# dS of two key chunks by one VectorE operation of 1000 columns

## The chip, the cores and the metric

The kernel runs on one core of a Trainium2 chip. The metric is the device time of one execution in microseconds (us), the median of several runs. The core has five engines with a queue each: TensorE (PE, its weight loads PEld), VectorE (DVE), ScalarE (ACT), GpSimd (POOL) and SyncE (SP), which here only issues DMAs. Matmuls write into PSUM, which has banks of 512 float32 columns per partition; DVE and ACT read it from there into SBUF.

## The reference

The program is one branch-former layer with its whole backward pass: attention on one side, a gated local branch with a depthwise convolution on the other, a merge of both, and the gradients of the input and of seven weights. There are 2 batches of 4000 tokens with 144 channels, in bfloat16. Cut to the part that matters here:

```python
B, T, D, K = (2, 4000, 144, 5)
qkv = jnp.einsum('btd,de->bte', _layernorm(x), w_qkv)
q, k, v = (qkv[..., :D].copy(), qkv[..., D:2 * D].copy(), qkv[..., 2 * D:].copy())
scores = jnp.einsum('btd,bsd->bts', q, k) * D ** (-0.5)
p = _softmax(scores, axis=-1)
attn = jnp.einsum('bts,bsd->btd', p, v)
...
_out, _vjp = jax.vjp(_f, x, w_qkv, w_att_out, w_mlp_in, dw_csgu, w_mlp_out, dw_merge, w_merge)
_grads = _vjp(grad_out)
```

The backward pass of the softmax is dS = P * (dP - delta), where dP is the gradient that arrives at P and delta is one number per query. It is this product that the change touches.

## The kernel before

The kernel handles the batches one after the other. For each there is a preparation (layer norm, transposes), the attention phase, in which forward and backward are fused, and a merge phase. The attention phase takes most of the time. It runs over 32 query tiles of 125 tokens (`PB`); the 4000 keys are 8 chunks of 500 columns (`CH`), handled as 4 pairs of chunks. In one step of the loop over `t` there are 8 slots:

- Slots 0 to 3 make the scores of tile `t` (`S_pair`). Four matmuls of 500 columns (L683, L684) fill a PSUM tile `ps` of two banks. One DVE operation over both banks (L688 for the first pair, L690 for the others) finds a running minimum of the negated scores, and one ACT operation (L691) writes the exponentials into `Pbuf`.
- After slot 3 `rescale` brings the first three pairs of chunks to a common maximum (two DVE operations L700, one of ACT L702), and a DMA transposes P into `PT` (L703). `Y_half` (L711) multiplies PT with the tokens in slots 2 and 3 of the next step.
- Slots 4 to 7 make dS of tile `t - 1` (`dP_pair`). Four matmuls (L733, L734) fill a `ps` tile with dP, and DVE subtracts delta, multiplies with P and writes dS into `Sbuf` (L739). At the end of the step a DMA transposes dS into `ST` (L859), which `Z_half` (L755) reads a step later.
- In most slots one `X_group` runs: matmuls (L794) of dS and P of tiles `t - 2` and `t - 3` into a PSUM tile `X`, and a DVE addition into `acc` (L800). Small pieces of the local branch (`units`) are spread over the slots by count.

The `ps` tiles of `S_pair` and `dP_pair` come from one pool with two buffers of two banks each; `X` and the small pieces share a pool of three buffers. The columns of P and dS lie in blocks of 125 with a stride of 128, so 500 columns are 4 rows of 125, and 1000 are 8. L739 stands in a loop over the two halves of the pair, each of which reads one bank:

```python
for h in range(2):
    c = 2 * c2 + h
    psrc = Pbuf[0:PB, i % NPB, c * 512:(c + 1) * 512]...
    sdst = Sbuf[0:PB, i % NDB, c * 512:(c + 1) * 512]...
    nc.vector.scalar_tensor_tensor(sdst, ps[:, h, 0:CH]..., DL[i][:], psrc, op0=ALU.subtract, op1=ALU.mult)
```

The source gives the order of the work by its slots. The framework in which the kernel is written puts the instructions into the engines' queues and sets the waits, and it may place an instruction ahead of an earlier one that is not ready by its reckoning. In the trace of before the two L739 of a pair follow each other directly in 214 of 256 pairs; in the other 42 another DVE operation stands between them. The tile `ps` is released as a whole.

Of the kernel before, what the change touches and what calls it, by code (L numbers as in the profile page):

```python
# [10 lines left out]
ALU = mybir.AluOpType  # L11
# [5 lines left out]
PB = 125  # L17
CH = 500
# [597 lines left out]
def phase_att(k, W, b, S, A, M):  # L616
    nc, tc = k.nc, k.tc
# [3 lines left out]
    NPB, NDB = 4, 3  # L621
    es_loc, es_sg = ExitStack(), ExitStack()
    with ExitStack() as es:
# [5 lines left out]
        Pbuf = ab.tile([128, NPB, GW], BF, name="Pbuf")  # L629
        Sbuf = ab.tile([128, NDB, GW], BF, name="Sbuf")  # L630
# [14 lines left out]
        QT, QB, RL, DL, YZ, ZN, ZT, NM, DHT = {}, {}, {}, {}, {}, {}, {}, {}, {}  # L645
# [24 lines left out]
        def pchunk(pb, c2):  # L670
            return Pbuf[0:PB, pb, c2 * 1024:(c2 + 1) * 1024]
# [55 lines left out]
        def dP_pair(i, c2):  # L727
            qt = QT[i]
            ps = ps_sg.tile([PB, 2, 512], F32, tag="sg")
            for h in range(2):  # L730
                c = 2 * c2 + h
                cs = slice(c * CH, (c + 1) * CH)
                nc.tensor.matmul(ps[:, h, 0:CH], qt[:, 2, :], xaTm[:, cs], start=True, stop=False)  # L733
                nc.tensor.matmul(ps[:, h, 0:CH], qt[:, 3, :], R[:, cs], start=False, stop=True)  # L734
            for h in range(2):
                c = 2 * c2 + h
                psrc = Pbuf[0:PB, i % NPB, c * 512:(c + 1) * 512].rearrange("p (a b) -> p a b", b=128)[:, :, 0:PB]
                sdst = Sbuf[0:PB, i % NDB, c * 512:(c + 1) * 512].rearrange("p (a b) -> p a b", b=128)[:, :, 0:PB]
                nc.vector.scalar_tensor_tensor(sdst, ps[:, h, 0:CH].rearrange("p (a b) -> p a b", b=PB), DL[i][:], psrc, op0=ALU.subtract, op1=ALU.mult)  # L739

        def last_tr(c2):

# [73 lines left out]
        for t in range(NB + 1):  # L816
# [9 lines left out]
            for s in range(8):  # L826
                if s < 4 and ok(t):
                    S_pair(t, s)
                if s >= 4 and ok(t - 1):
                    dP_pair(t - 1, s - 4)  # L830
# [630 lines left out]
```

## Time and profile before

| what | value |
|---|---|
| median of 3 runs | 1478.05 us (1475.49 to 1479.26) |
| the profiled execution, its own time | 1477.11 us |
| its span, first to last instruction | 1475.3 us |
| mean granted TensorE clock | 0.985 |
| busy: PE, DVE, ACT, POOL | 1377.6, 1217.1, 849.7, 282.0 us |
| attention phases in the span | about 60 to 660 us and 770 to 1373 us |

The profile is of one execution. A group of instructions is named by its line, engine, operation and the tiles that it writes and reads (out<-in), with its shape and count; behind the bar stand its busy time in us, the mean duration of one in ns, and the idle time of its engine just before such instructions, with what ended most of it ("<-PE ps L734" is the matmul of line 734). In a timeline the columns are start, duration, engine, line, operation; "x2" joins two neighbours into one row, and the bracket has the idle time of the engine before it. DVE operations overlap a little: the next one starts before the one before has quite ended, so an operation holds the engine for less than its duration.

### The profile page before, as it was taken

The numbers are of one execution on the slowest core, as the hardware profiler recorded it, in microseconds if no ns is written. First come the engines' busy times: TensorE is split into PE (matmuls) and PEld (weight loads), VectorE is DVE, ScalarE is ACT, GpSimd is POOL, SyncE is SP. The second block draws the span as 40 slices with busy tenths as digits, with TensorE's granted clock in tenths as the row PEclk, the third lists the DMA queues.
The fourth block names the chain that finished last, engine by engine and source line by source line (L and its number), as shares of the span: only waits on it lengthen the run. The fifth ranks groups of instructions, "written<-read, shape, count | busy, mean of one in ns | idle before, by whom it ended". The sixth has DMA issues, their size and how long they took to land. (4 is left out here: it accounts for less than half of the span.)

```text
span 1475.3 us, 39163 instructions
## 1 busy us (share of the span) xinstructions
PE 1377.6 (93%) x16184; PEld 1181.5 (80%) x16184; DVE 1217.1 (82%) x3060; ACT 849.7 (58%) x1538; POOL 282.0 (19%) x494
## 2 busy tenths in 40 slices
PE   2789999999999999997888999999999999999898
PEld 1568888888888888887885888888888888888797
DVE  6699888988898988887638998889898889888754
ACT  1666666666566656632637666666566656555182
POOL 8210111010111110026521112120101010101420
PEclk9899999999999999998999999999999999999999
DMA  3176667666666765578225776677667666677812
GB/s 101 31 144 121 121 121 122 120 122 117 118 115 113 119 118 111 107 138 209 62 56 104 138 122 113 111 121 124 119 123 121 121 121 121 116 117 124 218 35 64
DMA packets 559360, 170.44 MB, mean 116 GB/s; under 512 B 542443, under 2 KB 554093, under 8 KB 559136
## 3 DMA queue, kind: packets, MB, share of 16 engines
q1 hardware_dynamic: 553338, 155.43, 57.1%
q0 software_dynamic: 4768, 12.14, 3.2%
q8 instruction: 126, 2.06, 0.6%
q10 hardware_dynamic: 1076, 0.38, 0.1%
q14 instruction: 52, 0.43, 0.1%
HBM read 21.07 MB, written 14.16 MB: 24 GB/s over the span
## 5 line engine op out<-in xcount | busy, mean ns | idle before, releaser
L739 DVE SCALAR_TENSOR_TENSOR Sbuf<-ps,delta,Pbuf 125x500 bf16<-125x500 f32 x512 | 356.0, 731 | 28.2 <-PE ps L734 25.4
L794 PE MATMUL X<-QBs,Sbuf 125*125 125x144 bf16 x2048 | 303.1, 226 | 6.7 <-DVE acc L800 3.0
L794 PE MATMUL X<-QBs,Pbuf 125*125 125x144 bf16 x2048 | 302.1, 226 | 0.0
L794 PEld LDWEIGHTS <-Pbuf 125*125 125x125 bf16 x2048 | 262.1, 137 | 14.9 <-issue 10.3
L794 PEld LDWEIGHTS <-Sbuf 125*125 125x125 bf16 x2048 | 261.9, 137 | 7.7 <-DVE Sbuf L739 2.0
L800 DVE TENSOR_TENSOR acc<-X,acc 125x432 f32<-125x432 f32 x372 | 203.4, 550 | 33.0 <-PE X L794 31.9
L683 PE MATMUL ps<-xaT_m,qt 128*125 128x500 bf16 x512 | 194.6, 380 | 11.2 <-ACT Pbuf L691 9.9
L733 PE MATMUL ps<-xaT_m,qt 128*125 128x500 bf16 x512 | 192.7, 376 | 8.0 <-ACT Pbuf L691 5.7
L684 PE MATMUL ps<-R,qt 128*125 128x500 bf16 x512 | 194.0, 379 | 0.0
L734 PE MATMUL ps<-R,qt 128*125 128x500 bf16 x512 | 191.2, 373 | 0.0
L711 PEld LDWEIGHTS <-PT 125*125 125x125 bf16 x2048 | 147.9, 137 | 24.3 <-DMA PT<-Pbuf 6.5
L755 PEld LDWEIGHTS <-ST 125*125 125x125 bf16 x1984 | 144.2, 138 | 18.1 <-DMA ST<-Sbuf 0.6
L711 PE MATMUL yz<-xa_aug,PT 125*125 125x145 bf16 x2048 | 151.1, 227 | 4.1 <-DMA PT<-Pbuf 4.0
L755 PE MATMUL yz<-xa_aug,ST 125*125 125x144 bf16 x1984 | 147.8, 228 | 0.4 <-DMA ST<-Sbuf 0.4
L684 PEld LDWEIGHTS <-qt 128*125 128x125 bf16 x512 | 70.8, 138 | 33.3 <-issue 14.2
L734 PEld LDWEIGHTS <-qt 128*125 128x125 bf16 x512 | 69.8, 136 | 27.7 <-issue 8.2
L547 POOL TENSOR_TENSOR A_dwc<-l_fl,A_dwc 128x512 f32<-128x512 f32 (+2 forms) x48 | 35.7, 744 | 292.8 <-ACT l_fl L546 292.8
L688 DVE TENSOR_SCALAR_CACHE_REDUCE Pbuf<-ps 125x1000 bf16<-125x1000 f32 x64 | 76.6, 1197 | 14.5 <-PE ps L684 14.3
L733 PEld LDWEIGHTS <-qt 128*125 128x125 bf16 x512 | 70.0, 137 | 23.1 <-DVE Sbuf L739 2.7
L683 PEld LDWEIGHTS <-qt 128*125 128x125 bf16 x512 | 70.6, 138 | 21.9 <-issue 1.3
L759 ACT ACTIVATE zn<-yz,rl 125x144 bf16<-125x144 f32 x64 | 24.2, 378 | 108.5 <-PE yz L755 108.5
L417 POOL TENSOR_SCALAR l_a<-l_sq 125x576 bf16<-125x576 bf16 x32 | 21.4, 670 | 292.6 <-ACT l_sq L415 252.9
(807 smaller groups left out, 3055.1 us busy)
## 6 DMA issues: line engine op xcount, KB each, us to landing
Yn_d<-yn SPq DMA_DIRECT2D x64, 35.2 KB
Zn_d<-zn SPq DMA_DIRECT2D x64, 35.2 KB
ug_d<-ugr SPq DMA_DIRECT2D x32, 70.3 KB
xo<-in_x_dram SPq DMA_DIRECT2D x16, 140.6 KB
out_dram<-dxo SPq DMA_DIRECT2D x16, 140.6 KB
go_h<-in_grad_out_dram POOLq DMA_DIRECT2D x4, 504.0 KB, 6.8
Zn<-Zn_d SPq DMA_DIRECT2D x4, 504.0 KB
PT<-Pbuf SPq DMA_TRANSPOSE x64
```

Of the source, the lines that this page charges most:

```text
L547: nc.gpsimd.tensor_tensor(acc, fl[0:rows, 0:n], acc, op=ALU.add)
L683: nc.tensor.matmul(ps[:, h, 0:CH], qt[:, 0, :], xaTm[:, cs], start=True, stop=False)
L684: nc.tensor.matmul(ps[:, h, 0:CH], qt[:, 1, :], R[:, cs], start=False, stop=True)
L688: nc.vector.tensor_scalar(pdst, src, -1.0, None, op0=ALU.mult, op1=ALU.min, accum_out=nm[:, 0:1])
L711: nc.tensor.matmul(Y, PT[0:PB, j, 0:PB], xaa[:, j, 0:D + 1], start=(j == 0), stop=(j == NB - 1))
L733: nc.tensor.matmul(ps[:, h, 0:CH], qt[:, 2, :], xaTm[:, cs], start=True, stop=False)
L734: nc.tensor.matmul(ps[:, h, 0:CH], qt[:, 3, :], R[:, cs], start=False, stop=True)
L739: nc.vector.scalar_tensor_tensor(sdst, ps[:, h, 0:CH].rearrange("p (a b) -> p a b", b=PB), DL[i][:], psrc, op0=ALU.subtract, op1=ALU.mult)
L755: nc.tensor.matmul(Z, ST[0:PB, j, 0:PB], xaa[:, j, 0:D], start=(j == 0), stop=(j == NB - 1))
L759: nc.scalar.activation(zn[:, 0:D], Z, ACT.Copy, scale=RL.pop(i)[:])
L794: nc.tensor.matmul(X[:, jj, :], l, r, start=(n_ == 0), stop=(n_ == len(ops) - 1))
L800: nc.vector.tensor_tensor(av, X[:, 0:nj, :], av, op=ALU.add)
```

## The change

The loop over the two halves goes. One operation takes both banks of `ps`, both chunks of `Pbuf` and both of `Sbuf`: 1000 columns in 8 rows of 125. The matmuls and all other operations stay as they are in the source.

```diff
-            for h in range(2):
-                c = 2 * c2 + h
-                psrc = Pbuf[0:PB, i % NPB, c * 512:(c + 1) * 512].rearrange("p (a b) -> p a b", b=128)[:, :, 0:PB]
-                sdst = Sbuf[0:PB, i % NDB, c * 512:(c + 1) * 512].rearrange("p (a b) -> p a b", b=128)[:, :, 0:PB]
-                nc.vector.scalar_tensor_tensor(sdst, ps[:, h, 0:CH].rearrange("p (a b) -> p a b", b=PB), DL[i][:], psrc, op0=ALU.subtract, op1=ALU.mult)
+            psrc = pchunk(i % NPB, c2).rearrange("p (h a b) -> p h a b", h=2, b=128)[:, :, :, 0:PB]
+            sdst = Sbuf[0:PB, i % NDB, c2 * 1024:(c2 + 1) * 1024].rearrange("p (h a b) -> p h a b", h=2, b=128)[:, :, :, 0:PB]
+            nc.vector.scalar_tensor_tensor(sdst, ps[:, :, 0:CH].rearrange("p h (a b) -> p h a b", b=PB), DL[i][:], psrc, op0=ALU.subtract, op1=ALU.mult)
```

## The prediction

> **What bounds the kernel now.** I read the table of engines first, then the windows of the two attention stretches (about 100 to 656 us and 780 to 1373 us), because a share over the whole span mixes stages.
>
> ```profile
> PE 1377.6 (93%) x16184; PEld 1181.5 (80%) x16184; DVE 1217.1 (82%) x3060; ACT 849.7 (58%) x1538; POOL 282.0 (19%) x494
> L739 DVE SCALAR_TENSOR_TENSOR Sbuf<-ps,delta,Pbuf 125x500 bf16<-125x500 f32 x512 | 356.0, 731 | 28.2 <-PE ps L734 25.4
> ```
>
> ```profile
> 400.00:500.00 100.00, 98.18 (x1138) 83.90 (x1136) 88.63 (x210) 61.13 (x114) 13.51 (x21) 1.00 0.66 116
> ...
> 980.00:1080.00 100.00, 98.73 (x1156) 84.99 (x1155) 90.55 (x212) 61.91 (x113) 13.64 (x24) 1.00 0.71 124
> ...
> 1180.00:1280.00 100.00, 96.84 (x1124) 82.67 (x1122) 86.21 (x198) 63.36 (x116) 14.70 (x22) 1.00 0.61 113
> ```
>
> The windows' columns are stretch, length, busy PE, weight loads, DVE, ACT, POOL, granted clock, DMA share, GB/s. In attention PE is busy 97 to 99% at full clock, DVE 86 to 91%. So PE bounds, DVE is close behind, and L739, the operation that is changed, is DVE's largest item. What DVE saves counts only where PE waits for DVE. PE's ends are modelled, so I also took the starts of consecutive matmuls from the timeline: 500 columns follow each other at 0.21 us, 144 columns at 0.061 us. Between 80 and 656 and between 790 and 1373 us there are 112 gaps of over 0.06 us beyond that pace, together 41 us. 31 of them (11.8 us) close just after a DVE operation ends, 78 (27.4 us) just after an ACT operation ends. 41 us is all that can be won there.
>
> Next I asked what L739 waits for and who waits for it:
>
> ```profile
> L739 DVE SCALAR_TENSOR_TENSOR Sbuf<-ps,delta,Pbuf x512: 699/731/743, 80.9 to 1372.5; 125x500 bf16<-125x500 f32 x171
> ...
>   PE ps L734: 25.4, 40
> ...
>   PEld L733: 2.7, 6
> ...
>   PE ps L733: 1.8, 6
> ```
>
> and for a place where PE is seen waiting, by the timelines of DVE and PE:
>
> ```profile
> 204.54 0.74 DVE L739 SCALAR_TENSOR_TENSOR Sbuf<-ps,delta,Pbuf 125x500 bf16<-125x500 f32 x1
> 205.42 0.88 DVE L700 TENSOR_SCALAR Pbuf<-Pbuf,f 125x1000 bf16<-125x1000 bf16 x2
> 206.21 0.73 DVE L739 SCALAR_TENSOR_TENSOR Sbuf<-ps,delta,Pbuf 125x500 bf16<-125x500 f32 x1
> ```
>
> ```profile
> 205.31 0.38 PE L733 MATMUL ps<-xaT_m,qt 128*125 128x500 bf16 x1
> ...
> 205.94 0.37 PE L734 MATMUL ps<-R,qt 128*125 128x500 bf16 x1
> ...
> 207.00 0.43 PE L733 MATMUL ps<-xaT_m,qt 128*125 128x500 bf16 x1 [0.30 <-DVE Sbuf L739]
> ```
>
> Two things are seen here. The two halves of a pair are not adjacent in DVE's queue, though they are in the source: L700 stands between them. And PE's next use of the score buffer (207.00) is let go by the second half (206.21 + 0.73), not bank by bank.
>
> **Removed: 256 operations.** The halves cost 0.73 us each, but the next starts before one ends. From the timeline of an unbroken run:
>
> ```profile
> 452.27 1.37 DVE L739 SCALAR_TENSOR_TENSOR Sbuf<-ps,delta,Pbuf 125x500 bf16<-125x500 f32 x2
> 453.56 0.59 DVE L800 TENSOR_TENSOR acc<-X,acc 125x432 f32<-125x432 f32 x1
> ```
>
> A pair holds DVE 453.56 - 452.27 = 1.29 us. For 1000 columns no row shows this operation; the nearest is L690, same source tile, same output layout, also with one scalar per partition:
>
> ```profile
> 424.33 1.25 DVE L690 TENSOR_SCALAR_CACHE_REDUCE Pbuf<-ps,nm__6647 125x1000 bf16<-125x1000 f32 x1
> 425.51 0.08 DVE L690 DVE_READ_ACCUMULATOR Pbuf<-ps,nm__6647 125x1 f32 x1
> ```
>
> It takes 1.25 us and holds DVE 1.18 us. L688, without the scalar operand, takes 1.20 us. From above, two full halves would be 1.46 us. I take 1.25 and 1.18, since 0.73 + 500 columns at 0.96 per ns (from L690 against L739: 1.25 - 0.73 = 0.52 us) gives the same. Saved: 1.29 - 1.18 = 0.11 to 0.12 us a pair, in 256 pairs 28 to 31 us of DVE's time; by durations, 1.37 - 1.25, the same.
>
> **Moved: the start.** One operation over both banks needs all four matmuls. That costs nothing: in all 256 pairs the first half starts at or after the end of the fourth matmul (by 0.04 us in 54 of them, median 0.47 us), since the wait is for the tile. The two waits become one and no wait is added. **Moved: the end.** Adjacent halves end 0.12 us earlier as one. Of the pairs 42 have something between their halves (18 times L700, else L531, L432, L433, L502, L420, L800); there the merged operation ends earlier by that too: at 204.54 it would end at 205.79 in place of 206.94, and PE's gap at 207.00 (0.46 us beyond pace) would be gone, if the merged operation keeps the first half's place. Six gaps of this kind add to about 2.5 us. What stood between the halves waits 0.52 us longer (1.18 less the half's 0.65): L700 matters most, since the transpose of P follows it. That transpose is issued 0.12 to 1.5 us after L700 and mostly right after ACT's L702, and its 4.85 us end 4.7 us or more before the first matmul that reads it in all but the first three and the last tile of each half. So L700 is covered, except there. Sbuf's other readers, X two tiles later and the transpose at the tile's end, get it earlier.
>
> **The sum.** For each of the 112 gaps I counted the halves in DVE's unbroken run ahead of it, at 0.062 us each, never more than the gap itself. For the 31 gaps that DVE itself closes this is 4.2 us: the lower end. For all 112, as if each ACT operation that closes one had been late by DVE's backlog, it is 14.4 us: the upper end. ACT's exponentials do wait for DVE (L691 waits 92.8 us for L690 in the table of waits), but gaps closed by L702, L667, L488 or L448 are more ACT's own queue. I take 8 us, nearer to the lower end. The profiled execution took 1477.1 us (span 1475.3 and 1.8 around it): 1477.1 - 8 = 1469.1. The runs' median is 0.9 us above it, so 1470. About 0.3%, or 4.4 us, can be told from no change.
>
> **Rivals.**
> - Saved and not seen. PE is busy 98%, most gaps are closed by ACT, and DVE's 30 us just become DVE's idle time. Gain 0 to 4 us: about 1476. For it: waits of PE that name L739 are 1.8 and 2.7 us. Against it: broken pairs and long DVE runs ahead of gaps. 0.21.
> - Another order, and a worse one: slower. The halves stand apart in 42 pairs and in 16 the pair's matmuls are apart as well, so the queues' order is planned from readiness and assumed durations, not taken from the source. One operation with a new length may shift what follows on DVE, PE and ACT, and PE stalls in the same places in both halves of the program (0.77 us at 226.32, 0.75 at 339.62, each X behind acc), so an order counts twice. Price: per 100 us PE idles 1.3 us in the best window, 3.2 in the worst, 2.0 on the mean of the nine full windows. The worst all along 11.5 such stretches is +13 us: 1490 to 1491. The best is -8 us. It decides against the change once over 8 us of new gaps appear, say one of 0.13 us a tile over 64 tiles. 0.21.
> - Halves were worth having: slower by a little. What stood between them loses its early place: 42 times 0.52 us, 22 us of lateness. L700 is covered, which leaves L531 (8 pairs, it feeds PE's transposes) and L800 (2): 10 x 0.52 = 5 us if all of it arrives at PE and nothing is won, 1482. Against it: the first half has no reader of its own, by the 256 starts and by the release at 207.00. 0.07. A rule of the Trainium skill speaks for this case (Perfetto Trace Analysis, section Optimizing Scalar/DVE Operations): where Vector is not saturated but makes other engines idle, breaking up its operations may let work complete sooner. DVE at 86 to 91% with PE gaps behind it meets its condition, but in this trace what waits, waits for both pieces.
> - The operation over two banks and 8 rows costs two halves, 1.46 us or more. Then DVE holds 0.1 us more a pair, 26 us, and by the sum's reasoning up to 8 us are lost: 1486. L690 reads the same two banks in 1.25 us, so 0.03.
>
> **How the numbers follow.** The forecast has 0.48. Faster by over 0.3% is the forecast and a little of the first rival: 0.49. Within 0.3%: 0.21. Slower: 0.30. The forecast's own range is 1463 to 1474 (14.4 and 4.2 us). A better order on top of the upper end reaches 1458; the range goes to 1459, and upwards to the price of the worse order, 1490.
>
> **What would show it.** L739 appears 256 times, 1.25 us each, and DVE's busy time falls by 28 to 33 us. PE's busy time falls little; waits for L739 ahead of L733 go from 1.8 us to about nothing, and windows in attention show PE at 98.5% or more. Wrong if the operation takes over 1.3 us, if DVE's idle time grows by what it saved with PE's gaps still 41 us (first rival), or if new gaps stand ahead of L794, L683 or L711 with the queues in another order (second).

## The result, and the profile after

The changed kernel takes 1473.41 us (median of 12 runs, 1469.47 to 1476.66), the kernel before 1479.2 us (12 runs, 1474.72 to 1482.76). The ratio is 0.9965, with a 95% interval of 0.9952 to 0.9978: 5 us, or 0.35%, faster. That lies inside the prediction's range, 3.4 us above its forecast of 1470. The profiled execution took 1475.32 us (span 1473.5), 1.9 us more than the median, and that of the kernel before (1477.11) 2.1 us less than its median, so the two traces are only 1.8 us apart and show less than the whole gain. L739 has become L737, and of the lines behind it each number is two lower (L800 is L798, L794 is L792).

The table of engines and the costliest group of DVE, from the page of the changed kernel:

```profile
PE 1374.8 (93%) x16184; PEld 1182.3 (80%) x16184; DVE 1192.4 (81%) x2804; ACT 850.2 (58%) x1538; POOL 282.2 (19%) x494
...
L737 DVE SCALAR_TENSOR_TENSOR Sbuf<-ps,delta,Pbuf 125x1000 bf16<-125x1000 f32 x256 | 320.1, 1254 | 34.3 <-PE ps L734 32.5
```

DVE has 256 instructions less (3060 to 2804) and is busy for 24.7 us less. One operation takes 1.254 us on the mean. In its timeline it holds the engine for 1.16 to 1.17 us (451.29 to 452.46), against 1.29 for two halves:

```profile
451.29 1.25 DVE L737 SCALAR_TENSOR_TENSOR Sbuf<-ps,delta,Pbuf 125x1000 bf16<-125x1000 f32 x1
452.46 0.29 DVE L798 TENSOR_TENSOR acc<-X,acc 125x144 f32<-125x144 f32 x1
```

The next lines are three of the windows in attention, with the same columns as before:

```profile
400.00:500.00 100.00, 98.28 (x1135) 84.08 (x1134) 88.42 (x192) 62.62 (x114) 12.70 (x20) 1.00 0.68 122
...
980.00:1080.00 100.00, 99.30 (x1158) 85.28 (x1156) 88.16 (x188) 64.39 (x115) 13.89 (x25) 1.00 0.73 124
...
1180.00:1280.00 100.00, 96.27 (x1113) 82.14 (x1111) 84.47 (x182) 61.58 (x112) 14.33 (x22) 1.00 0.65 116
```

The best window is better than the best of before (99.30 against 98.73) and the worst is worse (96.27 against 96.84). PE's gaps in attention, counted as in the prediction (start to start of consecutive matmuls beyond their pace), fall from 41 us to between 38 and 39. The waits of L733 for this operation, 1.8 us before, have not gone:

```profile
who waited for it (us, times):
  PE ps L733: 2.0, 2
```

So a DVE relief nearly as large as forecast closed few of PE's gaps in this trace. The order of the queues shows why that can be: of PE's 16184 matmuls 823 stand at another place than before, and on DVE there are 245 places where the sequence differs, beyond the merged pairs themselves.

### The profile page after: what moved, and what is told of

The parts are those of the page before. It is cut to its first block, busy times and chain, and to the rows that moved or that the text cites. A ratio compares the mean times of both kernels' runs of the same rounds, so it can differ in the third digit from the quotient of the medians.

```text
span 1473.5 us, 38917 instructions
## 1 busy us (share of the span) xinstructions
PE 1374.8 (93%) x16184; PEld 1182.3 (80%) x16184; DVE 1192.4 (81%) x2804; ACT 850.2 (58%) x1538; POOL 282.2 (19%) x494
## 5 line engine op out<-in xcount | busy, mean ns | idle before, releaser
L737 DVE SCALAR_TENSOR_TENSOR Sbuf<-ps,delta,Pbuf 125x1000 bf16<-125x1000 f32 x256 | 320.1, 1254 | 34.3 <-PE ps L734 32.5
L792 PE MATMUL X<-QBs,Sbuf 125*125 125x144 bf16 x2048 | 302.6, 226 | 5.1 <-DVE acc L798 2.5
L792 PE MATMUL X<-QBs,Pbuf 125*125 125x144 bf16 x2048 | 301.6, 226 | 0.0
L792 PEld LDWEIGHTS <-Pbuf 125*125 125x125 bf16 x2048 | 262.0, 137 | 13.5 <-issue 9.4
L792 PEld LDWEIGHTS <-Sbuf 125*125 125x125 bf16 x2048 | 261.7, 136 | 4.9
L798 DVE TENSOR_TENSOR acc<-X,acc 125x432 f32<-125x432 f32 x372 | 203.6, 550 | 41.9 <-PE X L792 41.2
L733 PE MATMUL ps<-xaT_m,qt 128*125 128x500 bf16 x512 | 192.2, 375 | 9.4 <-ACT Pbuf L691 6.9
L711 PEld LDWEIGHTS <-PT 125*125 125x125 bf16 x2048 | 151.2, 139 | 22.1 <-DMA PT<-Pbuf 4.3
L711 PE MATMUL yz<-xa_aug,PT 125*125 125x145 bf16 x2048 | 154.2, 230 | 2.8 <-DMA PT<-Pbuf 2.8
L733 PEld LDWEIGHTS <-qt 128*125 128x125 bf16 x512 | 70.0, 137 | 21.1 <-issue 0.6
```

The lines of the kernel that those rows point to most:

```text
L711: nc.tensor.matmul(Y, PT[0:PB, j, 0:PB], xaa[:, j, 0:D + 1], start=(j == 0), stop=(j == NB - 1))
L737: nc.vector.scalar_tensor_tensor(sdst, ps[:, :, 0:CH].rearrange("p h (a b) -> p h a b", b=PB), DL[i][:], psrc, op0=ALU.subtract, op1=ALU.mult)
L792: nc.tensor.matmul(X[:, jj, :], l, r, start=(n_ == 0), stop=(n_ == len(ops) - 1))
L798: nc.vector.tensor_tensor(av, X[:, 0:nj, :], av, op=ALU.add)
```

## The experiments

Two theories. "Load": DVE holds each pair for 0.12 us less, and PE waits less for what DVE does next. "Order": the operation's new length made the framework place the instructions otherwise, and the time comes from that. Only the two together were in the changed kernel. To take them apart, the order of every queue was written out in the kernel, as edges of issue order between neighbours of one queue, which add no wait:

```diff
+def pin_order(tc):
+    ...
+    for e, rs in QUEUES.items():
+        q = [by[e][n] for a, c in rs for n in range(a, a + c)]
+        ...
+        for p, n in zip(q, q[1:]):
+            tc.add_manual_dep(n, p.name, info(), reason="order")
```

`QUEUES` holds a permutation for each engine, taken from the kernel before ("old order") or the changed one ("new order"). In every trace of such a kernel PE and DVE ran their instructions in exactly the order written out. All ratios below are to the kernel before, with 95% intervals; the times are medians.

**The changed kernel with its own order written out.** The control; no edit but the lines above.

> The changed kernel once more, with its own order written out for every queue in the way used for the other kernels. It shows whether the writing out alone changes anything: it should take the changed kernel's time, 0.3 to 0.4% below before, 1473 to 1475 us.

Measured: 0.9954 (0.9941 to 0.9966), 1473.1 us. As the changed kernel, within the intervals: writing the order out changes nothing that can be seen. The old order was not written out for the unchanged source, so for it there is no such control.

**One operation, old order.** The changed kernel's source; `QUEUES` from the kernel before, with the merged operation in place of the first half and the second half's place dropped.

> One operation of 1000 columns, but every engine's queue kept in the order of the kernel before (the merged operation at the first half's place). Theory 'load': the gain is DVE's shorter hold (0.12 us a pair) and the pairs no longer broken; then this is as fast as the changed kernel, about 0.4% below before, 1473 us, L739's place in DVE's busy time 25 to 33 us lower and PE's gaps (41 us) some 5 us smaller. Rival 'order': the gain comes from the new order of the queues; then this stays at before's time, within 0.2%.

Measured: 0.9942 (0.9927 to 0.9957), 1470.3 us. PE's gaps are some 35 us, 6 less than before. The operation alone is worth 8.6 us; nothing else moved, but for the second halves of the 42 broken pairs, which now run at the first half's place. By its median this is the fastest kernel in which nothing is left out, though its interval touches the changed kernel's.

**Two halves, new order.** The source of before; `QUEUES` from the changed kernel, with each merged operation replaced by its two halves.

> Two operations of 500 columns, adjacent, with every engine's queue in the order of the changed kernel. Theory 'load': DVE holds 0.12 us more per pair again, so the time is back near before, 1477 to 1480 us. Rival 'order': as fast as the changed kernel, 0.4% below before.

Measured: 1.0057 (1.0042 to 1.0071), 1487.3 us: 0.6% slower than before, which neither theory had. Load and order both count, with opposite signs. In the new order the merge is worth 14 to 15 us (1.0057 against 0.9965 or 0.9954). A part of it can be placed: near 169, 208, 886 and 925 us PE falls 0.92 us behind its pace at an L794 that waits for ACT's L667; with the merged operation in the same order it is 0.15. That is 3 of the 12 us between the two traces; the rest is not traced to places.

**Halves adjacent, old order.** The source of before; in the 42 broken pairs the second half is moved up behind the first.

> Two operations of 500 columns in the order of before, but the second half moved up directly behind the first in the 42 pairs where something stood between. DVE's load is that of before. If the broken pairs cost PE what the six gaps ahead of L733 show (2.5 us), 0.1 to 0.2% below before; if what stood between matters as much, no difference; if the halves apart are worth something, slower by up to 0.3%.

Measured: 1.0008 (0.9998 to 1.0017), 1480.4 us: no gain. This is also the closest partner of the second experiment, with the same order and two operations in place of one: 1.0008 against 0.9942 puts the shorter hold alone at 10 us. The place that the prediction showed tells why the closed gap brought nothing. These are the timelines of DVE, ACT and PE in this kernel:

```profile
205.30 1.39 DVE L739 SCALAR_TENSOR_TENSOR Sbuf<-ps,delta,Pbuf 125x500 bf16<-125x500 f32 x2
206.60 0.87 DVE L700 TENSOR_SCALAR Pbuf<-Pbuf,f 125x1000 bf16<-125x1000 bf16 x2
```

```profile
204.17 1.10 ACT L691 ACTIVATE Pbuf<-ps,nm__2898 125x1000 bf16<-125x1000 f32 x1 [0.29 <-DVE Pbuf L690]
205.16 0.37 ACT L723 ACTIVATE yn<-yz,rl 125x144 bf16<-125x144 f32 x1
205.43 0.53 ACT L725 ACTIVATE QBs<-qb,rl 125x288 bf16<-125x288 bf16 x1
...
206.44 1.12 ACT L702 ACTIVATE Pbuf<-Pbuf,f 125x1000 bf16<-125x1000 bf16 x1
207.45 0.50 ACT L524 ACTIVATE l_w<-gd,c,nc 125x144 f32<-125x144 bf16 x1
207.85 0.56 ACT L667 COPY qt<-pt 128x500 bf16<-128x500 bf16 x1
```

```profile
207.30 0.38 PE L733 MATMUL ps<-xaT_m,qt 128*125 128x500 bf16 x1
207.52 0.37 PE L734 MATMUL ps<-R,qt 128*125 128x500 bf16 x1
208.46 0.22 PE L794 MATMUL X<-QBs,Sbuf 125*125 125x144 bf16 x1 [0.57 <-ACT qt L667]
```

PE's gap ahead of L733, 0.46 us before, is gone, as argued. But the matmul that follows, L794, now stands 0.74 us behind its pace where it was 0.24: it waits for ACT's L667, which empties a tile of the pool that `X` shares, and ACT runs from L691 to L667 without a pause. The gap moved one step on. What starts that chain on ACT is L691's wait for DVE's L690.

**One operation, old order, at the second half's place.** As the second experiment, but in the 42 broken pairs the merged operation stands behind what was between the halves.

> One operation of 1000 columns in the old order, but at the place of the second half. It differs from the first place only in the 42 pairs that were broken: what stood between the halves now goes first, and the merged operation 0.5 to 1.3 us later. If DVE's shorter hold is what counts, as fast as the first place, 1470 us; if the earlier release of the score buffer in the broken pairs is a part of it, slower by the 2.5 us that six gaps showed, 1472 to 1473.

Measured: 1.0017 (1.0004 to 1.0030), 1480.3 us. The same instructions in the same queues but for 42 places, and the whole gain is gone, 10 us by the medians and 11 by the ratios. That is far more than either expectation. The same spot in the timelines of DVE and PE, first with the second half's place:

```profile
207.71 0.88 DVE L700 TENSOR_SCALAR Pbuf<-Pbuf,f 125x1000 bf16<-125x1000 bf16 x2 [0.86 <-ACT f L696]
208.50 1.25 DVE L737 SCALAR_TENSOR_TENSOR Sbuf<-ps,delta,Pbuf 125x1000 bf16<-125x1000 f32 x1
```

```profile
209.81 0.37 PE L733 MATMUL ps<-xaT_m,qt 128*125 128x500 bf16 x1 [0.69 <-DVE Sbuf L737]
```

and with the first half's place:

```profile
202.72 1.26 DVE L737 SCALAR_TENSOR_TENSOR Sbuf<-ps,delta,Pbuf 125x1000 bf16<-125x1000 f32 x1
203.90 0.87 DVE L700 TENSOR_SCALAR Pbuf<-Pbuf,f 125x1000 bf16<-125x1000 bf16 x2
```

```profile
204.72 0.38 PE L733 MATMUL ps<-xaT_m,qt 128*125 128x500 bf16 x1
204.93 0.37 PE L734 MATMUL ps<-R,qt 128*125 128x500 bf16 x1
```

L700 has to wait for ACT's `f` (0.86 us). The first half, or the merged operation at its place, runs in that time; behind L700 it sits and waits with it, and with it the score buffer that L733 needs. Gaps of 0.8 to 1.3 us ahead of L733, each ended by L737, stand at eight such places (near 171, 210, 304 and 629 us, and again 714 us later). Together they are 8.3 us, most of what was lost.

**Less of dS: where relief ends.** Two kernels leave out the second half of dS from the fourth tile on, for the fourth pair alone in the new order, and for all pairs in the old order:

```diff
-            nc.vector.scalar_tensor_tensor(sdst, ps[:, :, 0:CH]..., DL[i][:], psrc, ...)
+            nh = 1 if i >= NDB and c2 == 3 else 2      # or: 1 if i >= NDB else 2
+            nc.vector.scalar_tensor_tensor(sdst[:, 0:nh], ps[:, 0:nh, 0:CH]..., DL[i][:], psrc[:, 0:nh], ...)
```

> The changed kernel in its own order of the queues, with the second half of the fourth pair's dS left out from the fourth tile on (that part of dS is stale, so the gradients are not the reference's): 58 operations of 500 in place of 1000 columns, 58 x 0.53 = 31 us less for DVE, as much again as the change saved. Theory 'load', PE still waiting for DVE: about as much gain again, 4 to 8 us below the changed kernel, 1466 to 1470. Rival 'order', or DVE already off PE's path: within 2 us of the changed kernel, 1472 to 1475.

Measured: 0.9950 (0.9933 to 0.9967), 1471.9 us. Another 27 us of DVE's busy time taken away (1192.4 to 1165.3) bring 1 to 2 us over the changed kernel (0.9965, or 0.9954 with its order written out). The intervals overlap, so this can't be told from nothing; "load" had 4 to 8.

> The merged operation in the old order with the second half of every pair's dS left out from the fourth tile on (stale dS, so the gradients are not the reference's): 232 operations of 500 in place of 1000 columns, 123 us less for DVE. It bounds what any relief of DVE at this place can bring. Theory 'load': after the first 31 us brought 9 us, the rest brings less and less, since 27 of 41 us of gaps close with ACT: 1458 to 1466 us. If PE were still waiting for DVE one for one, below 1450; if DVE is off the path already, 1469 to 1471.

Measured: 0.9921 (0.9909 to 0.9933), 1467.0 us. In this order the merge took 26 us from DVE's busy time and brought 8.6 us; leaving out the halves takes another 105 (1190.8 to 1086.3) and brings 3.1, with intervals that just overlap. From the table of engines and the waits of this kernel, where L799 and L793 are the L800 and L794 of before:

```profile
PE 1375.2 (94%) x16184; PEld 1182.2 (81%) x16184; DVE 1086.3 (74%) x2804; ACT 849.8 (58%) x1538; POOL 280.8 (19%) x494
...
DVE acc L799 <- PE X L793: 102.6, 112, 8.6
```

DVE now waits for PE: 102.6 us ahead of the additions into `acc`, where it was 31.9 in the kernel before and 42.8 with the whole merged operation in this order. PE still has some 30 us of gaps, which less DVE time at this place did not take away.

**Which part of the new order costs.** The merged operation with queues from both kernels: by engine, and by stretch (the start of each attention phase, up to 130 us and from 740 to 842 us, against the rest; here GpSimd's queue stayed in the old order).

> One operation of 1000 columns; TensorE's queue in the order of the changed kernel, all other queues in the order of before. The merged operation in the old order took 1470.3 us, the changed kernel 1474. Theory 'PE': TensorE's places in the new order cost those 4 us; then 1474 us (0.4% below before). Rival 'others': the places on DVE and ACT cost them; then 1470 us (0.6% below before).

> The counterpart: TensorE's queue as before, DVE's, ACT's, GpSimd's and SyncE's as in the changed kernel. Theory 'PE': 1470 us. Rival 'others': 1474 us. If both this and the other one are slower than 1474, the queues only fit each other as a set.

Measured: 0.9988 (0.9976 to 1.0000) with PE's queue new and the others old, 1.0034 (1.0021 to 1.0046) the other way round. Both are slower than either order whole (0.9942 old; 0.9965 and 0.9954 new), though the first one's interval just touches the changed kernel's: the queues fit as a set, and neither PE's queue nor the other four hold the loss alone.

> One operation of 1000 columns. PE's, DVE's, ACT's and SyncE's queues in the changed kernel's order up to 130 us and from 740 to 842 us, that is where each attention phase starts; in the order of before elsewhere. Of the 4 us by which the changed kernel is behind the merged operation in the old order, its trace puts some 1 us into the start of the first phase and 2 us into that of the second. If the starts hold the loss: 1473 us. If the steady tiles hold it: 1470 us.

> The counterpart: the old order in the two starts, the changed kernel's order elsewhere. If the starts hold the loss: 1470 to 1471 us; if the steady tiles do: 1473 us.

Measured: 0.9953 (0.9941 to 0.9966) with the new order at the starts alone, 0.9991 (0.9981 to 1.0001) with the new order elsewhere. Both values expected for the second were wrong: it is slower than either whole order. Where the new order loses its 2 to 3 us stays open; parts of it do not add up.

## Why the prediction was right or wrong

- **The operation's price: right.** 1.254 us and 1.17 held, where 1.25 and 1.18 were taken from L690. Two banks and eight rows cost nothing more, so that rival is out. DVE's busy time fell by 24.7 us, a little under the 28 to 33 forecast, though the operation's own group fell by 35.9 (356.0 to 320.1). Most of the difference is overlap: the halves ran beside the ends and starts of their neighbours, time that the engine's busy time counts once, and 7 us less of it is left. The other operations' busy time rose by 4 us, which stays unexplained.
- **The start costs nothing: right.** In the trace of after the operation again never starts before the end of the fourth matmul; in 70 of 256 pairs it starts 0.04 us behind it. The median distance in the trace of before is 0.67 us, not the 0.47 of the prediction, which changes nothing.
- **The sum: right for what it counted, with luck.** It had 8 us, between 4.2 and 14.4, for a lighter DVE in the order of before. That experiment gave 8.6 us, and 11.7 us when nearly all of dS's second halves went, so the upper end was a fair bound in this order. The 8 was a choice between two far bounds, so that it met 8.6 is luck in part. That the changed kernel, at 1473.4 us, still lies in the forecast's own 1463 to 1474 is luck as well, for the sum had no term for the order.
- **The broken pairs: half wrong.** The six gaps ahead of L733 do close, but closing them alone brought no gain (1.0008): at four of the six places the wait for ACT's L667 took 0.4 to 0.5 us over. The term of 2.5 us had a second wait behind it that the prediction did not look for. With the merged operation in the old order the six close and no wait takes their place. And the condition beside it, "if the merged operation keeps the first half's place", was worth 10 to 11 us, not 2.5: the sign hung on it, and the prediction put no price of its own on its failing. In the changed kernel's order the operation stands ahead of what was between the halves in 40 of the 42 pairs. The condition was met, but the prediction gave no reason why it would be.
- **Rival "saved and not seen": out.** The merge is worth 9 to 10 us in one order (against before, and against adjacent halves) and 14 to 15 in the other.
- **Rival "another order": it came, beside the forecast and not in its place.** The order did change. With halves it costs 7 us (1.0057 against 1.0008, intervals apart); with the merged operation 2 to 3 us (0.9965 and 0.9954 against 0.9942; the intervals overlap, so this is likely and no more). The measured gain of 5 us is 8.6 less what the order took. The price range of the rival, -8 to +13 us from the windows, is about what orders did: the same instructions took from 0.9942 to 1.0034, which is 14 us.
- **Rival "halves were worth having": wrong as put.** Moving what stood between the halves behind both did no harm that shows (1.0008). What the halves had was the first one's place ahead of L700. The Trainium skill's sentence on breaking up operations (Perfetto Trace Analysis, section Optimizing Scalar/DVE Operations) was not borne out here: in both orders the broken-up form was slower, by 10 and by 14 to 15 us. The first piece did use time in which L700 would have waited for ACT (0.86 us at the place shown), but a merged operation at that place uses it as well.
- **What would show it: partly wrong.** 256 operations of 1.25 us came. Waits of L733 for the operation near nothing did not, which goes with the new order: in the old order with the merged operation the trace has none. PE at 98.5% or more in all windows did not come either, and there the order is not the whole cause, for in the old order three of the nine full windows stay below (98.4, 98.3 and 97.4%).

## What to carry to other kernels

When a framework orders the queues by its own reckoning, an edit is two changes: the operation, and an order that nobody chose. Write the old order out as issue-order edges and time the operation in it; here that version had the lowest median of all complete kernels. And before counting a closed gap as gain, look at the wait behind it on the next engine, and at what an operation would sit behind if it moved in its queue.

## What the runs showed that was not expected

With the same instructions, 42 places in one queue were worth 10 to 11 us of 1479, as much as the whole merge, which takes 26 us from VectorE's busy time, is worth in that order. And the saving has a sharp end: those 26 us gave 8.6 us, four times as much again gave some 3 us.
